# An attention-and-MLP kernel on one core: w_in loaded in three transfers of whole rows instead of six of half rows

## The chip, the cores and the metric

The kernel runs on one core of one Trainium2 chip. The metric is the device time of one execution in microseconds (us). Before the change the median of three runs is 234.35 us (234.19 to 235.34).

The core has a matrix engine (PE), three engines for elementwise work (DVE, ACT, POOL), a queue engine that only issues transfers (SP), and 16 DMA engines that carry out every transfer. A transfer is issued by an instruction on SP, ACT or POOL; SP's go through what the profile calls queue q1 (hardware), POOL's through q0 (software). Work of the two queues runs on the same 16 DMA engines.

## The reference, cut to what matters

```
for t in range(S):                                   # B=4, H=8, S=768, D=48
    state = f[t] * state + outer(k[t], v[t])         # f = sigmoid(f_logit), per batch and head
    y[t]  = q[t] @ state
x = y as [B*S, H*D]                                  # 3072 x 384
h = x @ w_in                                         # w_in: 384 x 2048, float32 in memory
g = (a0 + a1 h + a2 h^2 + a3 h^3) / (1 + |b0||h| + |b1| h^2 + 1e-6)
out = g @ w_out                                      # w_out: 2048 x 384
```

A gated linear attention gives x, and a two-layer MLP with a rational activation follows. All of w_in is needed for every row of x.

## The kernel before, in words

The work is cut into 12 units: 3 stretches of 256 time steps for each of 4 batches. For a unit the kernel loads f, k, q (float32, through SP) and v (cast to bf16 on the way, through POOL), takes exponentials and running sums of the gates (`ef`, `ls`, `cs`, `A`), scales k and q (`xa n 1` for k, `xa n 0` for q, on DVE, L315), transposes them (`T`), forms the scores (`sc`), masks them (`mk`, DVE, L358), forms y (`yi`, `yb`), copies y out as x (`ye`, ACT, L434), multiplies with w_in (`h`, PE, L455), and then goes through the rational activation and w_out.

There is no scheduler. The string `ORDER` at the head of the file is the program: its steps are issued from left to right, and each engine works off its own instructions in that order, waiting where data or a buffer isn't ready. A step such as `ld 1 q` loads q of unit 1; `h 0 0 4 @2` computes the first four of the sixteen 128-column blocks of h of unit 0; `wi 0 8` loads columns 0 to 8x128 of w_in.

`load_w_in` (L207 to L216) issues one transfer for each of three 128-row groups (kk = 0, 1, 2), so `wi 0 8` and `wi 8 16` are six transfers, all on POOL's queue. A group is made of four runs of 32 rows (one run for each pair of heads), which is why the source has the pattern `[96 * d_ff, HP], [d_ff, 32], [1, n]`: 4 times 32 rows of n numbers. The rows are read as float32 and written as bf16. With n = 1024 a row's part is 4096 bytes read and 2048 bytes written.

On POOL's queue the transfers of v for units 0 and 1 stand ahead of w_in. On SP's queue, in the same stretch, stand (in this order) `ld 2 f`, `ld 1 k`, `ld 1 q`, `ld 2 q`, `ld 3 f`, `ld 2 k`, `ld 4 f`, each 1024 pieces of 384 bytes. DVE's order in this stretch is: the steps of unit 0 up to `st 0 1`, then `xa 1 1` (needs k of unit 1), `xa 1 0` (needs q of unit 1), the scaling of the coefficients (L270), the two masks of unit 0 (`mk 0 0`, `mk 0 1`), and from there on the rest.

Of the kernel before, what the change touches and what calls it, by code (L numbers as in the profile page):

```python
# [19 lines left out]
ab_ b a; ld 0 f 0 2; cz 1; cu 0; ld 0 f 2 4; cz 3; cz 2; cz 0; ld 0 k 0 2; cu 1; ld 1 f; ld 0 q 2 4; ld 0 v; cm  # L20
ld 0 q 0 2; fa; ci; ef 0 0 2; ld 0 k 2 4; ld 1 v; si 0 0 @0; ef 0 2 4; ld 2 f; ls 0 0 2; ls 0 2 4; cs 0 0 2 @1
ab_ a a; ld 1 k; cs 0 2 4 @2; ef 1; A 0 0 0 2; A 0 1 0 2; A 0 1 2 4; ae 0 0 2; A 0 0 2 4; ls 1; xa 0 0 2 4
ld 1 q; xa 0 0 0 2; ae 0 2 4; cs 1 @3; xa 0 1 2 4; xa 0 1 0 2; T 0 2 4 @1; ae 1; A 1 0; ld 2 q; vm 0 1; wi 0 8
ic 0; A 1 1; Te 0 2 4; T 0 0 2 @2; ef 2; st 0 0; ld 3 f; si 0 1; ls 2; Te 0 0 2; sc 0 1 @1; wi 8 16; st 0 1
ld 2 k; cs 2 @3; xa 1 1; xa 1 0; sc 0 0 @2; A 2 1; fb; vm 0 0; T 1 @0; A 2 0; mk 0 0; ae 2; fr; mk 0 1
si 1 0 @3; ic 1; yi 0 1 @2; st 1 0; yb 0 2 4; Te 1; yb 0 0 2; ld 4 f; sc 1 0 @1; ye 0 s; ld 3 v; sc 1 1 @0
mk 1 0; si 1 1; vm 1 1; vm 1 0; h 0 0 4 @2; mk 1 1; ld 2 v; st 1 1; xa 2 0; h 0 4 8 @1; hy 0 0 4; ld 4 q
# [582 lines left out]
```

## Time and profile before

| What | us |
|---|---|
| median of 3 runs | 234.35 |
| the profiled execution's own time | 232.19 |
| its span, first to last instruction | 230.5 |
| DVE busy | 204.2 (89% of the span) |
| PE busy | 196.3 |
| ACT busy | 195.8 |
| POOL busy | 84.8 |

The profiled execution is 2.16 us below the median of the runs. The granted TensorE clock was 0.999 of full speed. DVE is the busiest engine; it is idle for most of the stretch from 16 to 24 us, and again for parts of the last 30 us. A share of busy time is an average over the whole span; the stretch that the change touches lies between 9 us, where the first of the six transfers of w_in is issued, and 31 us, where the last of them has landed and the first matmul with w_in runs.

### The profile page before, as it was taken

How to read it: one execution, taken by the hardware profiler on the slowest of the kernel's cores; microseconds unless marked ns; L12 is line 12 of the kernel's file. 1: busy time of each engine (PE TensorE's matmuls, PEld its weight loads, DVE VectorE, ACT ScalarE, POOL GpSimd, SP SyncE). 2: the span in 40 equal slices, each digit the busy share in tenths (PEclk: the TensorE clock that was granted, in tenths of full speed). 3: DMA queues.
4: the chain of work that ended last, by engine and by line, in shares of the span. 5: the costliest groups of instructions: out<-in, count | busy, mean ns of one | idle time of the engine just before them, and what ended most of it. 6: DMA issues, size and time to landing. Idle time of an engine off the chain costs nothing.

```text
span 230.5 us, 6995 instructions
## 1 busy us (share of the span) xinstructions
PE 196.3 (85%) x3112; PEld 141.8 (61%) x3112; DVE 204.2 (89%) x184; ACT 195.8 (85%) x183; POOL 84.8 (37%) x102
## 2 busy tenths in 40 slices
PE   0493599867999999899999988999996998899992
PEld 0362378646676777477767747767865675665550
DVE  5251788999999999999999999999999999989860
ACT  4751139999999999999999998999997995999960
POOL 7420030089408701733575394143370332311000
PEclk9999999999999999999999999999999999999999
DMA  6999999999996999999999899999973899998235
GB/s 139 221 218 186 187 201 218 251 193 147 179 215 129 165 176 274 263 231 254 275 221 240 213 165 179 149 240 184 164 149 70 170 179 196 205 204 167 74 81 124
DMA packets 64094, 43.19 MB, mean 187 GB/s; under 512 B 53696, under 2 KB 58816, under 8 KB 64064
## 3 DMA queue, kind: packets, MB, share of 16 engines
q0 software_dynamic: 22800, 23.87, 65.0%
q1 hardware_dynamic: 40976, 18.88, 34.9%
q8 instruction: 24, 0.39, 0.7%
q10 hardware_dynamic: 288, 0.00, 0.1%
q14 instruction: 6, 0.05, 0.1%
HBM read 25.17 MB, written 4.72 MB: 130 GB/s over the span
## 4 chain that ended last, share of the span: by engine, by line
DVE 45%; ACT 19%; DMA 14%; issue 11%; PE 6%; SPq 3%; DVEq 0%; ACTq 0%; POOLq 0%
DVE g L533 7%; DMA q<-in_q_dram 7%; DVE h L471 6%; DVE scm L358 6%; ACT lq L501 6%; DVE g L521 5%; ACT qi L506 4%; DMA z<-h 4%; PE hp L455 4%; DVE g L511 4%; DVE hy L516 4%; ACT hy L467 3%; SPq L204 3%; DVE z L475 3%; DMA g<-hy 3%
## 5 line engine op out<-in xcount | busy, mean ns | idle before, releaser
L455 PE MATMUL hp<-x,w_in_sb 128*128 128x256 bf16 x576 | 68.0, 273 | 4.0 <-ACT x L434 1.7
L542 PE MATMUL op<-w_out_sb,g 128*128 128x384 bf16 x384 | 69.2, 326 | 1.3 <-issue 0.7
L455 PEld LDWEIGHTS <-w_in_sb 128*128 128x128 bf16 x576 | 55.9, 98 | 15.7 <-issue 6.1
L467 ACT CAST hy<-hp 128x1024 bf16<-128x1024 f32 x48 | 49.2, 1073 | 4.1 <-PE hp L455 4.1
L542 PEld LDWEIGHTS <-g 128*128 128x128 bf16 x384 | 36.1, 98 | 25.5 <-issue 2.6
L501 ACT ACTIVATE lq<-z 128x2048 f32<-128x2048 bf16 x22 | 43.0, 1983 | 2.7 <-DMA z<-h 2.7
L506 ACT ACTIVATE qi<-lq 128x4096 bf16<-128x4096 f32 (+1 forms) x14 | 44.5, 3187 | 0.1
L525 POOL DMA_DIRECT2D g<-hy x19 | 18.2, 1105 | 51.3 <-ACT hy L467 21.8
L497 POOL DMA_DIRECT2D z<-h x16 | 15.4, 967 | 41.2 <-DVE z L475 11.8
L521 DVE TENSOR_TENSOR g<-g,h 128x4096 bf16<-128x4096 bf16 (+1 forms) x13 | 29.4, 2259 | 0.0
L358 DVE TENSOR_TENSOR scm<-sc,mask 128x1024 bf16<-128x1024 f32 x24 | 28.3, 1210 | 0.7 <-PE sc L350 0.7
L471 DVE TENSOR_TENSOR h<-hy 128x4096 bf16<-128x4096 bf16 (+1 forms) x13 | 27.5, 2116 | 1.1 <-ACT hy L467 1.1
L533 DVE TENSOR_TENSOR g<-g,qi 128x4096 bf16<-128x4096 bf16 (+1 forms) x14 | 27.7, 1978 | 0.9 <-ACT qi L506 0.8
L310 ACT ACTIVATE A<-cs 128x768 f32<-128x768 f32 (+1 forms) x26 | 20.3, 809 | 9.0 <-DVE qkp L315 9.0
L204 POOL DMA_DIRECT2D v<-in_v_dram x12 | 13.9, 1214 | 20.6 <-PE y L371 17.1
L315 POOL TENSOR_TENSOR qkp<-k,A 128x768 bf16<-128x768 f32 x9 | 18.4, 2049 | 6.6 <-ACT A L310 6.6
L329 PE MATMUL tp<-ident,qkp 128*128 128x128 bf16 x192 | 14.7, 234 | 6.8 <-DVE qkp L315 6.5
L511 DVE TENSOR_SCALAR g<-hy,a_sb 128x4096 bf16<-128x4096 bf16 x12 | 18.1, 1509 | 0.1
L315 DVE TENSOR_TENSOR qkp<-q,A 128x768 bf16<-128x768 f32 (+1 forms) x13 | 11.6, 898 | 6.8 <-ACT A L310 3.8
L329 PEld LDWEIGHTS <-qkp 128*128 128x128 bf16 x192 | 12.4, 105 | 8.5 <-DVE qkp L315 7.0
L516 DVE TENSOR_SCALAR hy<-hy,a_sb 128x4096 bf16<-128x4096 bf16 x12 | 16.8, 1402 | 0.0
L365 POOL COPY vmp<-v 128x128 bf16<-128x128 bf16 x24 | 14.5, 676 | 4.8 <-DMA v<-in_v_dram 3.6
(69 smaller groups left out, 252.6 us busy)
## 6 DMA issues: line engine op xcount, KB each, us to landing
g<-hy POOLq DMA_DIRECT2D x19, 512.0 KB, 7.7
z<-h POOLq DMA_DIRECT2D x16, 512.0 KB, 6.6
f<-in_f_logit_dram SPq DMA_DIRECT2D x11, 384.0 KB, 7.6
k<-in_k_dram SPq DMA_DIRECT2D x11, 384.0 KB, 7.4
q<-in_q_dram SPq DMA_DIRECT2D x11, 384.0 KB, 8.0
out_dram<-osb SPq DMA_DIRECT2D x22, 192.0 KB, 6.4
v<-in_v_dram POOLq DMA_DIRECT2D x12, 192.0 KB, 7.6
w_in_sb<-in_moe_w_in_dram POOLq DMA_DIRECT2D x6, 256.0 KB, 13.1
```

The costliest lines, as they stand in the source:

```text
L315: i = (nc.gpsimd if eng == "p" else nc.vector).tensor_mul(s["qk"][:, x, :, hh, 0:D], s["qk"[x]][:, hh].rearrange("p h i d -> p i h d"), s[ ...
L329: nc.tensor.transpose(t[:, x, i, p, :], s["qk"][:, x, i, 2 * p:2 * p + 2, :].rearrange("t h d -> t (h d)"), ident)
L358: return nc.vector.tensor_mul(t, s["sc", g].rearrange("s r a i t -> s (r a) (i t)"), mb)
L455: nc.tensor.matmul(t[:, m - m0, :].rearrange("f (j t) -> f j t", j=UB), w_in_sb[:, kk, m * P:(m + 1) * P], s["x"][:, :, kk, :], start=(kk ...
L467: nc.scalar.copy(fl(big(s, "hy"), m0, m1), fl(s["hp", m0], 0, m1 - m0))
L471: return nc.vector.tensor_mul(fl(big(s, "h2"), m0, m1), fl(big(s, "hy"), m0, m1), fl(big(s, "hy"), m0, m1))
L501: nc.scalar.activation(fl(lq, m0, m1), fl(big(s, "z"), m0, m1), AF.Ln, scale=regs[2], bias=1.0 + 1e-6)
L506: nc.scalar.activation(fl(qi, m0, m1), fl(lq, m0, m1), AF.Exp, scale=-1.0)
L511: return nc.vector.tensor_scalar(fl(big(s, "g"), m0, m1), fl(big(s, "hy"), m0, m1), a_sb[:, 3:4], a_sb[:, 2:3], op0=ALU.mult, op1=ALU.add)
L521: return nc.vector.tensor_mul(fl(big(s, "g"), m0, m1), fl(big(s, "g"), m0, m1), fl(big(s, "h2"), m0, m1))
L533: return nc.vector.tensor_mul(fl(big(s, "g"), m0, m1), fl(big(s, "g"), m0, m1), fl(qi, m0, m1))
L542: nc.tensor.matmul(s["op", g][:, j, 0:DM], big(s, "g")[:, m, C * j:C * j + C], w_out_sb[:, m, :], start=(s["on", j] == 1), stop=(s["on", j ...
```

## The change

`wi 0 8` and `wi 8 16` become one step, `wi 0 16`, at the place of the first. `load_w_in` is the same; it is now called once with n = 2048, so it issues three transfers, each of 128 whole rows (8192 bytes read and 4096 bytes written per row), instead of six of 128 half rows. The bytes moved are the same. All other steps stand in their old order; on POOL the only difference is three DMA instructions in the place of six.

```
-ld 1 q; ...; ae 1; A 1 0; ld 2 q; vm 0 1; wi 0 8
-ic 0; A 1 1; Te 0 2 4; T 0 0 2 @2; ef 2; st 0 0; ld 3 f; si 0 1; ls 2; Te 0 0 2; sc 0 1 @1; wi 8 16; st 0 1
+ld 1 q; ...; ae 1; A 1 0; ld 2 q; vm 0 1; wi 0 16
+ic 0; A 1 1; Te 0 2 4; T 0 0 2 @2; ef 2; st 0 0; ld 3 f; si 0 1; ls 2; Te 0 0 2; sc 0 1 @1; st 0 1
```

More of the change, by code (lines that the diff above doesn't have):

```diff
@@ L22 @@
 ab_ a a; ld 1 k; cs 0 2 4 @2; ef 1; A 0 0 0 2; A 0 1 0 2; A 0 1 2 4; ae 0 0 2; A 0 0 2 4; ls 1; xa 0 0 2 4
-ld 1 q; xa 0 0 0 2; ae 0 2 4; cs 1 @3; xa 0 1 2 4; xa 0 1 0 2; T 0 2 4 @1; ae 1; A 1 0; ld 2 q; vm 0 1; wi 0 8
-ic 0; A 1 1; Te 0 2 4; T 0 0 2 @2; ef 2; st 0 0; ld 3 f; si 0 1; ls 2; Te 0 0 2; sc 0 1 @1; wi 8 16; st 0 1
+ld 1 q; xa 0 0 0 2; ae 0 2 4; cs 1 @3; xa 0 1 2 4; xa 0 1 0 2; T 0 2 4 @1; ae 1; A 1 0; ld 2 q; vm 0 1; wi 0 16
+ic 0; A 1 1; Te 0 2 4; T 0 0 2 @2; ef 2; st 0 0; ld 3 f; si 0 1; ls 2; Te 0 0 2; sc 0 1 @1; st 0 1
 ld 2 k; cs 2 @3; xa 1 1; xa 1 0; sc 0 0 @2; A 2 1; fb; vm 0 0; T 1 @0; A 2 0; mk 0 0; ae 2; fr; mk 0 1
```

## The prediction

> **What bounds the kernel now.** I read the page's chain of work that ended last, then that chain in order of time, then DVE's timeline where the chain enters DVE, then the transfers by stretch, and last the busy times by stage.
>
> The page, chain by engine and line:
>
> ```profile
> DVE 45%; ACT 19%; DMA 14%; issue 11%; PE 6%; SPq 3%; DVEq 0%; ACTq 0%; POOLq 0%
> ```
>
> The chain in order of time (start, length, what):
>
> ```profile
> 6.59 2.19 SPq L204
> 8.79 0.04 issue
> 8.83 15.50 DMA q<-in_q_dram
> 24.33 0.02 issue
> 24.35 0.96 DVE qkp L315
> ```
>
> The chain starts on SP's queue, passes at 8.83 us into one transfer, q of unit 1, and stays there for 15.5 us. DVE's timeline says who waits (in brackets: idle time before, and what ended it):
>
> ```profile
> 20.38 0.96 DVE L315 TENSOR_TENSOR qkp<-k,A 128x768 bf16<-128x768 f32 x1 [4.03 <-DMA k<-in_k_dram]
> 24.35 0.96 DVE L315 TENSOR_TENSOR qkp<-q,A 128x768 bf16<-128x768 f32 x1 [3.02 <-DMA q<-in_q_dram]
> 25.23 0.74 DVE L270 TENSOR_SCALAR a_sb<-a_sb,sig 128x3 f32<-128x3 f32 x3
> 25.88 1.21 DVE L358 TENSOR_TENSOR scm<-sc,mask 128x1024 bf16<-128x1024 f32 x1
> ```
>
> `xa 1 1` waits for k of unit 1, `xa 1 0` for q; unit 0's masks, its y and the first h all stand behind. Why does a load of 384 KB take 15.5 us? The transfers from 13 to 31 us:
>
> ```profile
> DMA packets 7782, 3.36 MB, mean 187 GB/s; under 512 B 7012, under 2 KB 7012, under 8 KB 7780
> q0 software_dynamic: 3168, 1.58, 61.1%
> q1 hardware_dynamic: 4612, 1.74, 59.4%
> ```
>
> 7780 - 7012 = 768 packets are of 2 KB or more: the 6 x 128 half rows of w_in, written as 2048 bytes. Queue q0 has 3168, so 2400 others, tiny: 400 for each w_in transfer. 16 are completion marks, one per DMA engine; the remaining 384 are 32 each on 12 engines, if the 128 rows lie on only 4 engines, 32 rows each (the source is 4 x 32 rows). The trace's sixteen completion marks per transfer fit: of the first transfer, 12 come from 14.9 to 16.8 us and four from 19.7 to 20.9. k of unit 1 shows the same: 12 engines by 15.9 us, the rest at 16.4, 16.6, 17.9 and 20.4. So k waits on engines that hold w_in data. The stretch from 15.5 to 19 us, where w_in flows:
>
> ```profile
> DMA packets 564, 0.71 MB, mean 202 GB/s; under 512 B 276, under 2 KB 276, under 8 KB 563
> q0 software_dynamic: 292, 0.59, 89.4%
> q1 hardware_dynamic: 271, 0.10, 18.5%
> ```
>
> 287 w_in packets against 271 of q1: one for one. Nearest to a 4096-byte packet are the later accumulating transfers, here from 122 to 124 us:
>
> ```profile
> DMA packets 182, 0.40 MB, mean 200 GB/s; under 512 B 93, under 2 KB 93, under 8 KB 182
> q0 software_dynamic: 91, 0.36, 95.5%
> q1 hardware_dynamic: 91, 0.03, 9.8%
> ```
>
> 89 large packets against 91 of q1: again one for one, at twice the length. Last, busy times by stage (PE, PEld, DVE, ACT, POOL):
>
> ```profile
> 50.00:90.00 40.00, 37.61 (x665) 28.41 (x666) 40.00 (x32) 40.00 (x40) 20.02 (x23) 1.00 1.06 177
> 90.00:130.00 40.00, 38.54 (x619) 27.63 (x617) 40.00 (x32) 40.00 (x36) 19.72 (x18) 1.00 1.13 242
> 130.00:170.00 40.00, 36.97 (x683) 27.82 (x682) 40.00 (x30) 38.58 (x37) 19.85 (x22) 1.00 1.02 178
> ```
>
> DVE is busy 120.00 of 120 us, so a delay of DVE at 24 us has no idle time ahead in which to vanish.
>
> **The change part by part.** *POOL's issues.* Three instructions fewer of 657 ns: 2.0 us off POOL. Worth nothing: behind them stands one 0.30 us copy (12.91 us), then POOL is idle for 17.1 us until 30.31. If that cover went, only v of unit 4 would move.
>
> *The first matmul needs all of w_in, not half.* Before, the six transfers landed at 20.9, 22.1, 23.4 and 24.3, 29.9, 31.0 us, and the first h (31.17 us) needed the first three. After, it needs all three; below they land by about 28.4 us. x, which h also needs, comes at 30.6 and will be later. Nothing, with over 2 us of cover. Without it PE's h would wait, then the copy of h on ACT and the square on DVE. The second half is earlier, which nobody waits for. Three waits on PE go, and the software queue's semaphores are taken in other turns; the transfers waited for are long done. Nothing.
>
> *Packets.* Each engine with data now carries 32 packets of 4096 bytes in the place of 32 of 2048. Length of one: 89.4% x 16 x 3.5 us / 287 = 174 ns before; 95.5% x 16 x 2 us / 89 = 343 ns for the 4096-byte one, an accumulation within SBUF. Lower bound: twice 174 less one fixed part, which can't exceed a whole small q1 packet (120.2% x 16 x 1 us / 822 = 23 ns, from 12 to 13 us): 325. Upper: twice the turn of 195 ns (16 x 3.5 / 287, with q1's packet in it) = 390. I take 343, the only packet of this size. A group of 32 lengthens by 32 x (343 - 174) = 5.4 us at most; between 4.8 and 6.2 by the bounds.
>
> *What that does to k and q of unit 1.* During those 32 packets q1 gets 32 of its own through, as before, but in about 11.4 us (32 turns of 16 x 2 / 89 = 360 ns) instead of 6.2 to 6.5. On the first transfer's engines k lands at 20.4 + 5 = 25.4 us. The third transfer's last mark moves from 23.4 to 23.4 + 5.0 = 28.4 us (5.0 for 5.4, as only 12 engines read at once where 16 did). Before, q landed at 24.4, with the fourth transfer's last mark (24.3). That transfer is gone, so q is now held by the third: 28.4 us. From the other side: on the first transfer's engines q is through at 24.4 + 5.0, less 32 tiny packets that no longer stand between. One takes 16 ns: from 19 to 24.5 us q0 has 1436 of them and 146 of w_in in 55.7% x 16 x 5.5 = 49.0 us, and (49.0 - 146 x 0.174) / 1436 = 16 ns; 32 make 0.5 us: 28.9. I take 28.5, nearer the mark that holds the data: **+4.1 us** on `xa 1 0`. Lower bound: 4.8, less 0.5 for tiny packets, less 0.9 by which the third mark came before the fourth, less 0.3 if fewer reading engines turn at 187 ns (171 w_in packets on 8 engines from 25 to 29 us) in the place of 195: +3.1. Upper: +6.2.
>
> Here the Trainium skill's page "DMA: Bandwidth & Descriptors", section "Why a DMA increments its semaphore by 16 and not by 1", says that a transfer is split over the largest number of engines up to 16 that divides both sides' slowest dimension. By it 4 x 32 source rows go to four engines; the 400 tiny packets agree, and the sum is the one above. If all 16 shared the rows, it would be the rival "shared work" below.
>
> *Behind it.* `xa 1 0` starts at 28.5 instead of 24.35, and L270, the masks, y, x, h all follow. q of unit 2 stands next in q1's queue: 1024 packets at 822 per us, 1.3 us, so about 30 us, needed at 33.30 before and 37.2 after; f of unit 3 about 31.5, needed at 35.24 before. Both hidden. DVE's waits after 24.4 us (0.7 on PE, 1.1 and 1.1 on ACT) end with PE and ACT work that itself waits for DVE, so they move along and absorb nothing.
>
> Sum: 0 + 0 + 4.1 + 0. The profiled execution, 232.19 us, becomes 236.3; the median, 2.16 above it, 234.35 + 4.1 = **238.5**.
>
> **The rivals.** *Shared work (smaller loss).* If q's landing is set by the sum of work of all 16 engines: by then 384 packets of 343 ns replace the 512 of 174 ns that the four early transfers had, (131.7 - 89.1) / 16 = +2.7 us, less 400 tiny ones of 16 ns, 0.4: +2.3, 236.6 us. The four late marks of k speak against it.
>
> The same page, section "Rules for kernel authors", advises at least 1 MiB per DMA and merging small transfers. Here the trace can't yet show it.
>
> *Fewer transfers end sooner (faster).* As a mechanism here: tiny packets fall from 2400 to 1200, 1200 x 16 ns / 16 = 1.2 us less; if q waited for that sum and not for the data packets, it would land 1.2 us earlier: 233.1. Against it: q waits behind data on the full engines, whose count of bytes ahead of it rises.
>
> *q1 overtakes (not slower).* If q1 gets three or more of its packets through per long packet, then 96 pass in 32 turns, k and half of q on the first transfer's engines, all of q on the third's, and q lands at about 24.5: 234.4. The point that decides is three for one. The rows say 91 to 89 and 271 to 287.
>
> *The change doesn't do what it says.* If each row is still cut into two packets of 2048 bytes, k lands as before, but each full engine holds 64 turns of 195 ns, 6.2 us more behind which q is taken one for one: q's 64 packets end with the third transfer's data, 28.5 to 29.6 us; +4.1 to +5.2, 239.0.
>
> *Longer packets (larger loss).* At 390 ns or beyond, from the cast: +5.2 to +6.2, 240.0.
>
> **How the numbers follow.** Forecast (+3.1 to +5.2): 0.62. Cut rows: 0.08. Shared work: 0.11. Longer packets: 0.10. q1 overtakes: 0.05. Fewer transfers end sooner: 0.04. A change of 0.5% (1.2 us) is about what a measurement of this kernel can tell from none. Faster 0.04, same 0.05, slower 0.91. Range 236.4 to 240.5: from shared work to the upper bound; it leaves out the last two and some of the tails, under 2 in 10.
>
> **What would show it.** 384 packets of 4096 bytes and about 1200 tiny ones on q0; three w_in transfers landing by 28.4; DVE waiting for k until about 25.4 and for q until about 28.5; the first h near 35; from there the same order with the same durations. Wrong, if q1 moves several packets per long one (k still at 20.4), if q lands within 1 us of 24.4, or if DVE's later idle shrinks by the shift.

## The result

The changed kernel takes 242.09 us in the median (240.96 to 243.48, 4 runs) against 234.27 (234.08 to 235.34, 4 runs): 1.0327 times as long, 95% interval 1.0262 to 1.0392. That is 7.8 us more, where +4.1 was forecast and the range ended at +6.2. The profiled execution took 240.96 us, its span 239.3 (before: 232.19 and 230.5), so the two profiles differ by 8.8 us.

The chain in order of time, changed kernel, its start (start, length, what):

```profile
8.85 22.74 DMA q<-in_q_dram
31.59 0.02 issue
31.62 0.96 DVE qkp L315
```

The same transfer, issued at the same time, now holds the chain for 22.7 us instead of 15.5. DVE's timeline:

```profile
28.13 0.96 DVE L315 TENSOR_TENSOR qkp<-k,A 128x768 bf16<-128x768 f32 x1 [12.19 <-DMA k<-in_k_dram]
31.62 0.96 DVE L315 TENSOR_TENSOR qkp<-q,A 128x768 bf16<-128x768 f32 x1 [2.53 <-DMA q<-in_q_dram]
...
43.89 0.69 DVE L475 TENSOR_SCALAR z<-hy 128x2048 uint16<-128x2048 uint16 x1 [2.37 <-ACT hy L467]
```

k of unit 1 is used at 28.13 us (20.38 before), q at 31.62 (24.35). Of q's sixteen completion marks four come by 21.3 us and twelve between 29.9 and 31.6 (before: all sixteen between 22.0 and 24.3), so q waits on the twelve engines that hold w_in. The first bit mask of the activation, L475, runs at 43.89 (35.38). So 7.27 of the 8.8 us are lost by the time that q has come, another 1.24 between there and the first bit mask, and 0.3 in all the rest of the kernel.

The transfers from 13 to 31 us, and from 16 to 26:

```profile
DMA packets 4364, 2.65 MB, mean 147 GB/s; under 512 B 3979, under 2 KB 3979, under 8 KB 4363
q0 software_dynamic: 1584, 1.58, 62.9%
```

```profile
DMA packets 1003, 1.40 MB, mean 140 GB/s; under 512 B 731, under 2 KB 731, under 8 KB 1002
q0 software_dynamic: 271, 1.11, 70.4%
q1 hardware_dynamic: 731, 0.28, 38.3%
```

4363 - 3979 = 384 long packets, with 1584 - 384 = 1200 tiny ones: the counts that the prediction named. But 271 long packets in 10 us on 12 engines are one every 443 ns on each engine, and one took 70.4% x 16 x 10 us / 271 = 416 ns. The transfers moved 140 GB/s in this stretch, less than the 202 of the half rows from 15.5 to 19 us, which lay on 16 engines.

Last, the first h in both kernels. First before, then after (ns min/median/max; first and last start):

```profile
L455 PE MATMUL hp<-x,w_in_sb x24: 272/273/418, 31.2 to 34.0; 128*128 128x256 bf16 x24
```

```profile
L455 PE MATMUL hp<-x,w_in_sb x24: 272/421/421, 38.4 to 42.5; 128*128 128x256 bf16 x24
```

Most of these matmuls became slower. The stages of the changed kernel (PE, PEld, DVE, ACT, POOL, then the granted clock, the DMA share and GB/s):

```profile
18.50:28.50 10.00, 0.00 (x0) 0.00 (x0) 0.37 (x1) 0.00 (x0) 0.00 (x0) 0.64 1.02 135
28.50:31.50 3.00, 1.04 (x8) 0.77 (x8) 0.59 (x1) 0.81 (x1) 0.00 (x0) 0.50 1.10 190
31.50:38.40 6.90, 5.10 (x150) 3.88 (x151) 5.96 (x9) 1.69 (x3) 0.82 (x1) 0.50 1.08 252
```

PE does nothing for the 10 us in which it waits for k, and the granted clock is at half when the first h begins. It is tempting to blame the longer wait, as the same rows for the kernel before say 1.00. But its trace has no record of the clock ahead of 31.9 us, and the rows count a stretch without a record as 1.00. The matmuls themselves tell the clock. Here are eight transposes before, after, and in an experiment (`pair_half_hold`, below) where the clock is on record as 1.00:

```profile
21.39 1.03 PE L329 MATMUL tp<-ident,qkp 128*128 128x128 bf16 x8 [3.18 <-DVE qkp L315]
```

```profile
29.15 1.04 PE L329 MATMUL tp<-ident,qkp 128*128 128x128 bf16 x8 [12.28 <-DVE qkp L315]
```

```profile
17.22 0.62 PE L329 MATMUL tp<-ident,qkp 128*128 128x128 bf16 x8
```

1.03 us is the time at half clock: the kernel before ran at half clock here as well, and the 0.999 given above for its whole execution is too high. What differs is when the full clock comes back. By the clock records of the two traces that is at 31.9 us before, 0.7 us after the first h began, and at 41.7 in the changed kernel, 3.3 us after.

### The profile page after: what moved, and what is told of

It reads as the page before. It is cut to its first block, busy times and chain, and to the rows that moved or that the text cites. A ratio compares the mean times of both kernels' runs of the same rounds, so it can differ in the third digit from the quotient of the medians.

```text
span 239.3 us, 6989 instructions
## 1 busy us (share of the span) xinstructions
PE 197.1 (82%) x3109; PEld 142.7 (60%) x3112; DVE 204.2 (85%) x184; ACT 195.8 (82%) x183; POOL 82.9 (35%) x99
## 4 chain that ended last, share of the span: by engine, by line
DVE 32%; DMA 16%; PE 15%; issue 15%; ACT 11%; POOL 5%; SPq 3%; POOLq 0%; DVEq 0%; ACTq 0%
DMA q<-in_q_dram 10%; PE op L542 9%; DVE scm L358 5%; DVE h L471 5%; PE hp L455 5%; DMA z<-h 5%; DVE g L533 4%; DVE g L521 3%; SPq L204 3%; DVE g L511 3%; ACT hy L467 3%; DVE z L475 3%; ACT lq L501 2%; ACT qi L506 2%; DVE qkp L315 2%
## 5 line engine op out<-in xcount | busy, mean ns | idle before, releaser
L455 PE MATMUL hp<-x,w_in_sb 128*128 128x256 bf16 x576 | 69.3, 276 | 4.6 <-ACT x L434 2.1
L455 PEld LDWEIGHTS <-w_in_sb 128*128 128x128 bf16 x576 | 56.7, 99 | 15.8 <-issue 6.7
L497 POOL DMA_DIRECT2D z<-h x16 | 15.5, 968 | 41.9 <-PE sv L417 8.5
L471 DVE TENSOR_TENSOR h<-hy 128x4096 bf16<-128x4096 bf16 (+1 forms) x13 | 27.6, 2120 | 1.4 <-ACT hy L467 1.4
L204 POOL DMA_DIRECT2D v<-in_v_dram x12 | 14.0, 1222 | 29.9 <-PE y L371 26.5
L315 POOL TENSOR_TENSOR qkp<-k,A 128x768 bf16<-128x768 f32 x9 | 18.4, 2046 | 6.7 <-ACT A L310 6.7
L315 DVE TENSOR_TENSOR qkp<-q,A 128x768 bf16<-128x768 f32 (+1 forms) x13 | 11.5, 888 | 6.3 <-ACT A L310 3.8
L475 DVE TENSOR_SCALAR z<-hy 128x4096 uint16<-128x4096 uint16 (+1 forms) x13 | 14.8, 1138 | 2.4 <-ACT hy L467 2.4
## 6 DMA issues: line engine op xcount, KB each, us to landing
w_in_sb<-in_moe_w_in_dram POOLq DMA_DIRECT2D x3, 512.0 KB, 20.7
```

Of the source, the lines that this page charges most:

```text
L315: i = (nc.gpsimd if eng == "p" else nc.vector).tensor_mul(s["qk"][:, x, :, hh, 0:D], s["qk"[x]][:, hh].rearrange("p h i d -> p i h d"), s[ ...
L455: nc.tensor.matmul(t[:, m - m0, :].rearrange("f (j t) -> f j t", j=UB), w_in_sb[:, kk, m * P:(m + 1) * P], s["x"][:, :, kk, :], start=(kk ...
L471: return nc.vector.tensor_mul(fl(big(s, "h2"), m0, m1), fl(big(s, "hy"), m0, m1), fl(big(s, "hy"), m0, m1))
```

## The experiments

Two things were to be explained: why the long packets cost 443 ns a turn and not 360, and what the last 1.2 us are. The theory was the prediction's own, "long packets": q1 gets one packet through per w_in packet on the engines that hold w_in. Its rival, "placement", said that the loss comes from crowding the data on 12 engines.

**The same engines, short packets (cut_rows).** w_in lies in two halves in the on-chip memory, so that each row is two packets (and `h` reads it accordingly):

```
-w_in_sb = consts.tile([P, KD, d_ff], BF16)
+w_in_sb = consts.tile([P, 2, KD, d_ff // 2], BF16)
-  dma_start(out=w_in_sb[:, kk, m0*P:m1*P], in_=AP(..., ap=[[96*d_ff, HP], [d_ff, 32], [1, n]]))
+  dma_start(out=w_in_sb[:, :, kk, :], in_=AP(..., ap=[[96*d_ff, HP], [d_ff, 32], [n//2, 2], [1, n//2]]))
```

> Three transfers as in the changed kernel, on the same engines, but each row as two packets of 2048 bytes (w_in lies in two halves in the on-chip memory). Theory 'long packets': q1 gets one packet through per w_in packet, and the 4096-byte ones take far longer than twice; cut, 64 turns of about 195 ns stand on each full engine: k of unit 1 back at 20 to 21 us, q at 28.5 to 29.5, span about 235 (before 230.5, changed 239.3). Rival 'placement': the loss comes from putting all data on 12 engines, whatever the packet's size: k stays at 26 to 28 us, q at 31, span 239.

Median 237.67 us, 1.012 (1.006 to 1.019) times its kernel before; span 236.1.

```profile
18.24 0.96 DVE L315 TENSOR_TENSOR qkp<-k,A 128x768 bf16<-128x768 f32 x1 [1.82 <-DMA k<-in_k_dram]
28.50 0.96 DVE L315 TENSOR_TENSOR qkp<-q,A 128x768 bf16<-128x768 f32 x1 [9.30 <-DMA q<-in_q_dram]
```

k comes even before 20 us, q at 28.5 as expected. k alone proves little, because it scatters: it was used at 28.13 us in the changed kernel, but at 21.70 and 23.13 in `warm_pe` and `warm_pe2` (below), which leave these transfers as they are. q scatters less (31.62, 34.02, 32.34). Read by q, the packet's length is only part of the loss: 64 short packets on an engine hold q back 4.15 us, 32 long ones on the same engine 7.27.

**Whole rows over all engines (spread_rows, pair_whole).** In `spread_rows` each transfer has 32 rows of one group; in `pair_whole` the 32 partitions of one run of rows with all three groups:

```
-for kk in range(KD):
-    dma_start(out=w_in_sb[:, kk, m0*P:m1*P], in_=AP(offset + 32*kk*d_ff + m0*P, [[96*d_ff, HP], [d_ff, 32], [1, n]]))
+for a in range(HP):
+    dma_start(out=w_in_sb[32*a:32*a+32, :, m0*P:m1*P], in_=AP(offset + 96*a*d_ff + m0*P, [[d_ff, 32], [32*d_ff, KD], [1, n]]))
```

> Whole rows as in the changed kernel, but twelve transfers of 32 rows each, which divide over all 16 engines: 24 packets of 4096 bytes on each engine and no tiny ones. Theory 'long packets': 24 turns of 450 ns are 10.8 us, so w_in ends about 25 us, k then and q about 26, span about 232; if the long turn of 450 ns came from four engines working into the same partitions, 24 x 360 ns, q at 24 to 25, span 230.5 to 231. Rival 'placement': q no later than before, span 230 or less.

> Whole rows again, in four transfers, one for each run of 32 partitions, each with the rows of all three groups: 24 packets of 4096 bytes on every one of the 16 engines, no tiny ones, and no wait between the issues. Theory 'crowded engines': the changed kernel lost because 32 long packets stood on each of 12 engines at a turn of 450 ns; here 24 turns of 348 ns (the turn seen with twelve transfers, packets of 322 ns) are 8.4 us, w_in ends about 22 us, q of unit 1 lands about 24.3, span 230.5 to 231.5. Rival 'long packets as such': k and q land as late as in the changed kernel, 28 and 31 us, span 239.

`spread_rows`: median of ten executions 233.56 us against 234.37 of before in the same round, which is a factor of 0.997; the interval on record, 0.990 (0.986 to 0.995), rests on the five shortest of the ten, so a gain isn't shown. q was used at 24.42 us. Some of its twelve issues on POOL stood behind waits for earlier w_in transfers (one of 2.2 us), which the form with four avoids. `pair_whole`: 233.66 us, 0.998 (0.994 to 1.002), span 231.1, k used at 22.80 and q at 24.70. Its transfers from 15 to 21 us:

```profile
DMA packets 653, 1.29 MB, mean 215 GB/s; under 512 B 370, under 2 KB 370, under 8 KB 652
q0 software_dynamic: 330, 1.16, 95.4%
q1 hardware_dynamic: 322, 0.12, 11.5%
```

282 long packets against 322 of q1 (a few of these are completion marks), a turn of 16 x 6 / 282 = 340 ns, and at most 95.4% x 16 x 6 / 282 = 325 ns for one packet. A whole row isn't slow, and isn't harmful in itself: 24 of them on each of 16 engines cost nothing that can be measured against the kernel before.

**Why a crowded long packet takes 416 ns (skew_reads, one_group).** Two ideas: the twelve engines read from addresses in step, or three of them write into the same 32 partitions (groups kk = 0, 1, 2 of one run of rows go to the same partitions). `skew_reads` shifts the source, so that the values of w_in are no longer right:

```
-offset + 32*kk*d_ff + m0*P,                 ap=[[96*d_ff, HP], [d_ff, 32], [1, n]]
+offset + 32*kk*d_ff + (KD - 1 - kk)*640,    ap=[[96*d_ff - 160, HP], [d_ff, 32], [1, n]]
```

> The changed kernel with each of its three transfers, and each run of 32 rows in it, reading from an address shifted by a few hundred numbers (the values of w_in in the chip are then wrong; sizes, engines, partitions and order are the same). It asks why a 4096-byte packet took 420 ns in the mean and not the 322 of the shortest. Theory 'reads in step': the twelve engines read at multiples of 256 KB from one another, and collide; shifted, packets go to 330 ns, k at about 24.5 us, q at 28.5, span 235.5. Rival 'writes into the same partitions' or another cause: packets stay at 420, k near 28, q near 31.5, span 239 to 241.

Median 241.67 us, 1.033 (1.026 to 1.039); q used at 33.26 us. From 16 to 26 us:

```profile
DMA packets 920, 1.21 MB, mean 121 GB/s; under 512 B 691, under 2 KB 691, under 8 KB 919
q0 software_dynamic: 228, 0.93, 68.8%
```

228 packets, 68.8% x 160 / 228 = 483 ns each: no shorter, so shifts of this size (at most 7040 bytes against one another, less than one row) don't help. Larger ones were not tried. Nor is 483 longer than without the shift: by the same rows the unshifted transfers took 451 ns a packet in `warm_pe2` and at most 507 in `warm_pe`. `one_group` leaves only group 0 in its old form and sends the rest later, over all engines:

```
-wi 0 16                     # kk = 0, 1, 2, four engines each
+wi 0 16                     # kk = 0 only
+wr ^m                       # kk = 1, 2: four transfers over 16 engines, after `xa 1 1` (m)
```

> Only the first of the three whole-row transfers is left in its place and form (32 packets of 4096 bytes on each of 4 engines); the other two groups' rows go in four transfers over all engines, issued only after k of unit 1 has been used. It asks whether a long packet is slow on an engine that works alone in its 32 partitions. Theory 'three in one place': with one transfer no two engines write into the same 32 partitions, packets take 322 to 330 ns, the turn is about 350 ns and k lands at 24 to 25 us. Rival 'one engine into 32 partitions': they take 400 ns and more even so, and k lands at 27 or later. The span (w_in's rest comes late) is about 237 to 240 in either case.

k was used at 22.90 us, q at 26.02; the median is 239.33 us, as w_in's rest comes late. From 14 to 24 us, with group 0 on its four engines:

```profile
DMA packets 1993, 1.15 MB, mean 115 GB/s; under 512 B 1872, under 2 KB 1872, under 8 KB 1992
q0 software_dynamic: 295, 0.49, 25.8%
```

120 long packets, a turn of 4 x 10 / 120 = 333 ns, at most 25.8% x 160 / 120 = 344 ns for one. So an engine alone in its 32 partitions is not slow with long packets; three groups at once are. Sharing 32 partitions isn't enough by itself, though: each transfer of `pair_whole` writes one run of 32 partitions from all 16 engines, at 325 ns a packet at most. Whether it matters that three engines go through the same partitions row by row, or that 12 engines each hold a run of rows of their own, these runs can't tell: in `one_group` both are gone, in `pair_whole` too.

**The clock (warm_pe, warm_pe2).** 90, then 100 extra matmuls on PE, first ahead of the transposes of unit 1, then earlier:

```
+def wm(n, times): for _ in range(times): matmul(unit(n)["cs", 0][:, 1, 384:512], ident, Us)
-... cs 2 @3; xa 1 1; ...
+... cs 2 @3; wm 2 100; xa 1 1; ...         # warm_pe2
```

> The changed kernel with 90 extra matmuls (identity times a constant, into an unused part of a PSUM tile, read by nobody) on PE ahead of the transposes of unit 1, to fill most of PE's wait for k from about 18 to 27 us. Theory 'clock': of the 8.8 us that the changed span lost, 7.3 are the wait for q and 1.2 the first h at half clock (24 matmuls in 4.18 us for 2.94); filled, the granted clock stays at 1.0 and the span is 238.0. Rival: the half clock costs nothing in the end, span 239.3.

> The changed kernel with 100 extra matmuls on PE (identity times a constant, into an unused part of a PSUM tile, read by nobody), now ahead of the scores of unit 0, so that they run from about 17.7 us and not only after k has come. Theory 'clock': the granted clock stays at 1.0 over the first h, its 24 matmuls take 2.9 us and not 4.2, and DVE's wait at the first bit mask (L475) is 1.1 and not 2.4 us. Rival: the first h takes 4.2 us and the wait 2.4 as in the changed kernel.

Neither settled it. In `warm_pe` (241.71 us) the extra matmuls had to wait for `A 2 1`, which reads the same tile and itself waits for k. In `warm_pe2` (242.04 us) the clock was 1.00 from 19 to 24 us, as meant, but PE then stood idle for most of the time until 32, and the first h ran at 0.58 of the clock with 24 matmuls of 417 ns. What the profiles do show, set side by side, one execution each (the return of the full clock is taken from the traces' clock records):

| kernel | full clock back, us after q was used | q used to first bit mask, us |
|---|---|---|
| before | 7.5 | 11.03 |
| `skew_reads` | 7.6 | 11.05 |
| `pair_whole` | 7.9 | 11.19 |
| `pair_half` (below) | 8.0 | 11.26 |
| `cut_rows` | 8.8 | 11.66 |
| `spread_rows` | 9.2 | 11.83 |
| `warm_pe` | 9.4 | 11.95 |
| changed | 10.1 | 12.27 |
| `warm_pe2` | 10.5 | 12.47 |

In all nine the first h starts 6.8 us after q was used, at half clock, and each us by which the full clock comes later costs about half a us. So the 1.24 us are the clock's. But they are not shown to be the change's: `skew_reads` loads q behind the same crowd and waits for it longer than the changed kernel, and loses nothing. What sets the moment of the return is open. The recorded stretches of full or half clock inside the traces are whole multiples of 3.41 us, which suggests that the clock is set anew at fixed beats and that the difference between 7.5 and 10.5 us is largely chance; no run tests that.

**Letting k and q ahead (hold_half, pair_half, pair_half_hold, pair_whole_hold).** If w_in's packets hold k and q up, they can be issued later, as nobody needs w_in before x. In `hold_half` the six transfers of before wait for `st 0 1` on DVE:

```
-... vm 0 1; wi 0 8
-... sc 0 1 @1; wi 8 16; st 0 1
+... vm 0 1
+... sc 0 1 @1; st 0 1 !m; wi 0 8 ^m; wi 8 16
```

> The kernel before (six transfers of half rows), but they are issued only after the second state update of unit 0 on DVE (about 16.3 us), so that k and q of unit 1 run ahead of them. Theory: q of unit 1 lands at 16 to 17.5 us and DVE goes on then; w_in's first half lands about 24.5 to 26 and becomes what the first h waits for; the second half lands about 31 to 33, needed about 31. Span 224 to 227. Rival: what was gained at q is lost again at w_in, span 230.

> Half rows over all 16 engines, not held: each engine has 48 packets of 2048 bytes in q1's way instead of 32 or 64 on some. Theory: k at 18.5 to 20 us, w_in through by 23, q at 23 to 24.3: span 229.5 to 230.5, so spreading alone gives next to nothing and the gain of the held kernel comes from letting k and q ahead. Rival: spreading is most of the gain, q below 20 us, span 227.

> Half rows over all 16 engines (eight transfers, four for each half, 24 packets of 2048 bytes per engine in each half), issued only after the first state update of unit 0 (14.9 us), so that k and q of unit 1 go ahead of them. Theory: q lands at 16.7 us as in the held kernel with six transfers; w_in's first packets at 17.5, its first half at 22.5 to 24, the second at 27 to 29; the first h at 23.5 to 24.5 in the place of 31.2, and the span falls to 223 to 225. Rival: the loads of units 2 and 3, now behind w_in, become the wait, and the span stays at 229 or above.

> As the kernel with held half rows over all 16 engines, but whole rows in four transfers: 24 packets of 4096 bytes per engine from about 17.9 us. Theory: spread and behind q, the row's length no longer hurts q (16.9 us), packets take 322 ns; but all of w_in must land before the first h: 17.9 + 24 x 348 ns = 26.3, with marks 26.5 to 27.5, so the first h starts 2 to 3 us later than with halves (24.5) and the span is 227.5 to 229. Rival: same as with halves, 225.9.

`hold_half`: q is used at 16.69 us, 7.7 earlier, but the first bit mask runs at 35.43, where it ran at 35.38 before: w_in's third transfer lands only about 30 us, so the wait moved from DVE's L315 to PE's first h. 233.5 us, 0.995 (0.991 to 0.999); the rival held. `pair_half`, spread and not held: k at 18.34, q at 24.89, 233.24 us, 0.997 (0.992 to 1.002); spreading alone gives nothing measurable. Both together, `pair_half_hold` (spread, and held behind `st 0 0`):

```profile
17.08 0.95 DVE L315 TENSOR_TENSOR qkp<-q,A 128x768 bf16<-128x768 f32 x1
...
30.74 0.69 DVE L475 TENSOR_SCALAR z<-hy 128x2048 uint16<-128x2048 uint16 x1 [3.77 <-ACT hy L467]
```

Median 228.49 us, 0.980 (0.976 to 0.984) of before, span 225.9: the first h starts at 24.48 us, as soon as w_in's first half is there. `pair_whole_hold`, the same with whole rows: 231.64 us, 0.989 (0.981 to 0.997), span 230.1; its last w_in transfer landed about 29 us, and the first h began at 29.3. I had expected a loss of 2 to 3 us against halves; it is 4.2 in span. This is the price of the coupling that the prediction had costed at nothing because x came later still: once q is early, whole rows make the first h wait for all of w_in.

**The clock once more (held_filled).** The first h of `pair_half_hold` ran at 0.55 of the clock. Three fillings of PE's gaps, in an unused corner of the state's PSUM tile:

```
-si 1 0 @3; ic 1; yi 0 1 @2; ...  yb 0 0 2; ...           mk 1 0; si 1 1; ...
+si 1 0 @3; ic 1; yi 0 1 @2; wm 1 14; ...  yb 0 0 2; wm 1 10; ...  mk 1 0; si 1 1; wm 1 10; ...
```

> The fastest kernel so far (half rows over 16 engines, held behind unit 0's first state update) with 34 extra matmuls of 128 columns on PE, in three gaps between 19 and 24.5 us, into an unused part of a PSUM tile that nobody reads. In that kernel the granted clock was 0.55 during the first h, whose 24 matmuls took 5.2 us. Theory 'clock': the halving comes from PE's gaps just before; filled, the clock stays at 1.0, the first h takes 2.9 us, and the span falls from 225.9 to 223.6 to 224.4. Rival: the clock halves all the same, or the extra matmuls delay PE's own work by as much as they save; span 225.5 to 227.

The first h, `pair_half_hold` and then `held_filled`:

```profile
L455 PE MATMUL hp<-x,w_in_sb x24: 318/418/418, 24.5 to 29.3; 128*128 128x256 bf16 x24
```

```profile
L460 PE MATMUL hp<-x,w_in_sb x24: 269/272/273, 26.1 to 28.6; 128*128 128x256 bf16 x24
```

The clock stayed at 1.00 from 20 to 30 us (0.50 to 0.55 from 23 us on without the filling) and the first h took 2.8 us in the place of 5.2. So in this kernel the halving does come from PE's gaps. Little of it reached the end: in this execution w_in's first half came at 26.1 and not 24.5 us, the first bit mask ran at 29.97 (30.74), and the span is 226.7. Median 228.09 us, 0.974 (0.968 to 0.980); its interval overlaps that of `pair_half_hold`, so a gain over it isn't shown. Both are faster than either of the two kernels of this case.

## Why the prediction was wrong

The direction, the place and the mechanism were right; one term of the sum was too small, and another, put at zero, came out at 1.24 us in the two profiles.

- *Packets on four engines, 32 each, one for one with q1.* Held: 384 long and 1200 tiny packets; the four late marks of the first transfer moved from about 20 us to between 27.6 and 28.7; spreading the rows (`pair_whole`) brought q back to 24.7. One for one can be checked by an estimate: of the 731 packets that q1 moved from 16 to 26 us, about 460 belong to the four engines without w_in (by the early marks of the two q loads, 20.7 to 21.3 and 27.0 to 27.2 us), which leaves about 270 for the other twelve, against 271 of w_in. The rule of the Trainium skill on the number of engines (page "DMA: Bandwidth & Descriptors", section "Why a DMA increments its semaphore by 16 and not by 1") agrees with all of these.
- *The length of a packet: the step that failed.* I took 343 ns, from accumulating transfers that spread over all 16 engines, with 390 as the upper end. Measured were 416 ns, a turn of 443 in the place of 360: 32 x 83 ns = 2.7 us more, of the 3.1 by which q was late: it was used at 31.6 us, not at 28.5. (k, forecast for 25.4, was used at 28.13, but at 21.70 and 23.13 with the same transfers in `warm_pe` and `warm_pe2`.) The lower bound of 325 was the right value, but for engines that don't crowd (325 and 344 at most in `pair_whole` and `one_group`). I had carried over a row of the right size from the wrong placement, and allowed nothing for three groups at a time.
- *"All follow", in the old order with the old durations.* Missed by 1.24 us: the first h ran at half clock for 3.3 us and not 0.7. PE's row in the sum was zero without a reason. But half clock was there before the change too, and `skew_reads` pays nothing with an even longer wait, so the 1.24 us belong to the two executions that were profiled and aren't shown to belong to the change. The Trainium skill's page "TensorE: Matmul & The Clock Gate", section "Part 1: The HAM clock gate (the "warmup" mystery)", says that the clock halves after an idle window of about 3.4 us. The traces that record a fall in a wait of PE are near that: it comes from 1.9 us (`warm_pe`) to 4.3 us (changed kernel) after PE's last matmul.
- *POOL's three issues, the semaphores, the loads behind q.* Zero, as said: the remaining 195 us of the kernel differ by 0.3. (The 37.2 us at which q of unit 2 would be needed comes to 37.4 by the forecast's own shift; it is covered either way.)
- *All of w_in before the first h.* Zero here, as said (last mark at 31.1 us, first h at 38.4), with the cover named; `pair_whole_hold` shows it without the cover.
- *The rivals.* "Longer packets" came nearest: with 390 ns it ended at +6.2, against +7.8 measured; its cause, the cast, was wrong, since the same cast took 325 ns at most when spread. "Cut rows" was run as a kernel of its own: q at 28.5 us and span 236.1, 5.6 over before, where +4.1 to +5.2 was worked out. "Shared work" as a kernel, `pair_whole`, cost +0.35 us at q and not +2.3. The Trainium skill's page "DMA: Bandwidth & Descriptors", section "Rules for kernel authors", advises at least 1 MiB per DMA and merging small transfers. Here the merge to 1 MiB (128 rows of 8192 bytes) was the slower one on twelve engines, and with the rows spread, the size of a transfer did not show: 233.66 us with four of whole rows, 233.24 with eight of halves, all under 1 MiB.

The sum as it came out: 7.3 (32 turns of 443 ns instead of 195 are 7.9 us, an estimate that leaves out what the fourth transfer had cost) + 1.2 for the clock's late return + 0.3 = 8.8 between the profiled executions. Against the medians it is 7.8; the profiled execution of before lies 2.1 us below its median and that of after 1.1. How much of the 1.2 us is in the medians is not known.

## What to carry to other kernels

A transfer's cost to others is read from what each DMA engine has in its queue: count data packets and tiny ones, look at whether all sixteen completion marks come together, and ask whose small packets must pass between the large ones. A packet's duration is only good for the placement in which it was measured. The first matmuls after a pause of PE need a range of their own: here one and the same stretch took from 11.0 to 12.5 us, by when the full clock came back. And a granted clock of 1.00 is worth checking against the spacing of like matmuls.

## What the runs showed that I had not expected

- Long packets on crowded engines lost bandwidth outright: 140 GB/s with whole rows on 12 engines, 174 with half rows on the same engines (`cut_rows`, 19 to 25 us), 215 with whole rows on 16. Three groups at a time took 416 to about 500 ns a packet, one group 344 at most; half rows in the same crowd about 172 (an estimate, (71.3% x 96 us less 195 tiny ones of 16 ns) / 380, from `cut_rows`, 19 to 25 us). The cause within that is open.
- The granted clock halves on less than one long pause: in `pair_half_hold` PE was busy for 1.1 of 2 us from 20 to 22, and the clock was 0.50 from 23 us on; 34 small matmuls in the gaps kept it at 1.00.
- The kernel's early loads had 5 to 6 us to give: w_in behind k and q of unit 1, and spread over all engines in halves, is 2.0% faster than before.
